# Routing of the last query items and the first expert's tokens in an attention, mixture-of-experts and softplus kernel

## The chip, the core and the metric

The kernel runs on one core of a Trainium2 chip. The metric is the device time of one execution in microseconds (us); runs of the kernel before and after the change are compared.

## The reference, cut to what matters

Three layers follow one another: a linear attention with exponential random features (4 batches, 8 heads, 576 positions, head size 64, 128 features), a mixture of experts that sends each of the 2304 tokens to one of 8 experts, and a dense layer with softplus.

```python
logits = x @ w_gate
expert_idx = np.argmax(logits, axis=1)
probs = np.exp(logits - logits.max(-1, keepdims=True))
probs /= probs.sum(-1, keepdims=True) + 1e-09
gate_w = probs[np.arange(N), expert_idx]
for e in range(E):
    mask = expert_idx == e
    h = np.maximum(x[mask] @ w1[e], 0.0)
    out[mask] = gate_w[mask, None] * (h @ w2[e])
```

Here x is the attention's output. The weight of the chosen expert is 1 / (sum of exp(logit - max) + 1e-9), as its own exponential is 1.

## The kernel before, in words

**Items.** Attention works through 20 items, numbered 0 to 19, of 256 tokens (`nr` 2) or 128 (`nr` 1): items 0 to 4 are the keys of the first two batches, 5 to 9 their queries, 10 to 14 and 15 to 19 those of the other two. The loop over `n` (from 950) runs item n's transposes and projections on TensorE (PE) beside the products of item n - 1. `at(step, slot, ...)` puts later steps of an item in a slot of a coming turn. A query item ends in products `nm` (`q_product`, 661) in PSUM banks of the tag `acc`, of which there are three; VectorE (DVE) divides them by their denominators `rc` into the token rows and, for the gate, into `lgp`.

**Routing.** Each query item goes through three steps. `route_pick` (702) sums the gate's logits `lg`, takes their maximum `rmx`, the differences `dl`, the candidates `cand`, their highest `cm` and the one-hot choice `oh`, all tiles of 128 x 16 or less in SBUF, on DVE; then it adds `oh` to the running count `run`, on GpSimd (POOL), for the last two items on DVE. `route_gate` (743) takes the exponential of `dl` on ScalarE (ACT), sums it, adds 1e-9 (L749), inverts (L750), and stores the token rows with their weight to `x_tok` in DRAM by a DMA on the queue of SyncE (SP). `route_rank` (874) multiplies `oh` by a triangle and the running counts by ones on PE (`rk`, L877 to L879), which gives each token's slot `sl` (L884) in its expert's list; POOL scatters the token's number into `id_slot` in DRAM by an indirect DMA (L906).

**The passage to the first expert.** The first expert (the fullest by items 5 to 9, chosen midway) starts before the last lists are written. `read_first` (772) reads its part of `id_slot` into `ids_0`, at the end of turn 18, behind the scatter of item 16. Item 17's tokens are added without DRAM: `add_first` (777) builds a one-hot `s0` of the slots on DVE (L782), multiplies token numbers by it on PE (`pid`, L786) and adds the result to `ids_0` on DVE (L789, L790). `gather_first` (793) then has POOL gather the rows by three indirect DMAs (L796) into `xg_0`; they also wait for item 17's store of `x_tok`. Items 18 and 19, the `tail`, never pass through DRAM for the first expert: their rows are split in two parts, `tail_h` (ACT, L752) and `tail_l` (DVE, L738), and multiplied by one-hot matrices `tail_s` of their slots in `first_tail` (810; L820, L823), which are built on ACT for item 18 (L889, L891) and on DVE for item 19 (L893). `first_split` (849) adds the gathered rows by products with diagonals of their weights (L859 on ACT, L863 on PE) into the same four PSUM tiles and splits the sum for the first expert's matmuls (L1069 to L1071). `fill` (803) puts zero products on PE in between: 4 and 4, then 3.

**What sets the order.** The text is one stream of instructions; the Tile framework gives every engine its own list in an order that its planner works out from estimated durations, with semaphores where data pass between engines. Within an engine's list, and in SP's and POOL's queues of DMAs, everything goes in that order: a waiting entry holds what is behind it. `behind(a, b)` makes the planner put a after b. From the first expert on, PE multiplies without pause by weights that SP's queue fetches.

## Time and profile before

| | |
|---|---|
| median of 3 runs | 831.66 us (830.14 to 833.51) |
| profiled execution | 830.93 us, span 829.2 us |
| mean granted clock of PE in it | 0.995 |
| busy share of the span | PE 98%, DVE 58%, ACT 57%, POOL 27% |
| attention's last product ends, first expert's first product starts | about 171.3 us, 182.1 us |

A span is the time from the first to the last instruction of an execution. Busy time is read per engine; idle time of an engine that nobody waits for costs nothing. "PEld" is PE's loading of the stationary operand, which overlaps its products. [...] "SPq" marks DMA issues of SP's queue.

### The profile page before, as it was taken

What the parts mean: (1) busy time and instruction counts of PE and PEld (TensorE: products, weight loads), DVE (VectorE), ACT (ScalarE), POOL (GpSimd) and SP (SyncE); (2) the same over time, 40 slices, a digit from 0 to 9 for tenths busy, and PEclk for the clock granted to TensorE, in tenths of its full rate; (3) what the DMA queues carried; (4) which work ended last, traced back from release to release, by engine and by line L of the source; (5) the groups of instructions that cost most, each with busy time, mean ns of one, the idle gap of its engine ahead of it and who ended that gap; (6) DMA issues with size and microseconds to landing.
All of it is one profiled execution on the core that took longest, in us unless ns stands there. A gap on an engine that the chain in (4) does not pass through costs nothing.

```text
span 829.2 us, 14048 instructions
## 1 busy us (share of the span) xinstructions
PE 813.3 (98%) x5121; PEld 756.8 (91%) x5123; DVE 484.5 (58%) x1038; ACT 473.4 (57%) x1051; POOL 227.7 (27%) x391
## 2 busy tenths in 40 slices
PE   8999999999999999999999999999999999999995
PEld 6999999979999999999999999999999999999994
DVE  6778877878777678787587666432232232222221
ACT  4787558847545545556456655664454455445442
POOL 7987898641110110110144233210000001001001
PEclk9999999999999999999999999999999999999998
DMA  9941164237777787889553220120010001001001
GB/s 258 205 131 59 33 179 160 97 102 213 221 248 246 247 272 257 276 267 311 193 157 122 77 103 1 51 102 1 1 39 38 1 1 40 1 0 39 1 1 40
DMA packets 80428, 99.29 MB, mean 120 GB/s; under 512 B 16616, under 2 KB 61832, under 8 KB 80356
## 3 DMA queue, kind: packets, MB, share of 16 engines
q1 hardware_dynamic: 76612, 88.53, 34.4%
q0 software_dynamic: 3744, 9.82, 3.5%
q8 instruction: 42, 0.69, 0.4%
q14 instruction: 30, 0.25, 0.2%
HBM read 78.59 MB, written 19.76 MB: 119 GB/s over the span
## 4 chain that ended last, share of the span: by engine, by line
PE 59%; issue 35%; POOL 2%; DVE 1%; ACT 1%; DMA 1%; SPq 0%; POOLq 0%; ACTq 0%; DVEq 0%
PE a L1069 7%; PE a L1070 7%; PE a L1071 7%; PE y L1069 4%; PE y L1071 4%; PE y L1070 4%; PE kvacc L607 3%; PE nm L670 3%; PE pj L552 2%; PE pj L556 2%; PE pj L555 2%; PE o L1366 2%; PE o L1363 2%; PE o L1368 2%; PE tq L654 2%
## 5 line engine op out<-in xcount | busy, mean ns | idle before, releaser
L1351 DVE SCALAR_TENSOR_TENSOR ab<-a,ab 128x384 f32<-128x384 f32 x96 | 53.4, 556 | 163.2 <-ACT ab L1350 163.1
L1069 PE MATMUL a<-yh,w 128*128 128x384 f32 x384 | 130.5, 340 | 0.0
L1071 PE MATMUL a<-yh,w 128*128 128x384 f32 x384 | 129.9, 338 | 0.0
L1070 PE MATMUL a<-yl,w 128*128 128x384 f32 x384 | 129.7, 338 | 0.0
L1366 PE MATMUL o<-w,gh 128*128 128x512 f32 x288 | 115.0, 399 | 0.0
L1363 PE MATMUL o<-w,gh 128*128 128x512 f32 x288 | 114.3, 397 | 0.0
L1368 PE MATMUL o<-w,gl 128*128 128x512 f32 x288 | 113.3, 394 | 0.0
L1348 ACT ACTIVATE ab<-a 128x384 f32<-128x384 f32 x96 | 47.0, 490 | 115.7 <-PE a L1071 115.7
L577 ACT ACTIVATE ph<-pj,nb 128x128 f32<-128x128 f32 x288 | 82.8, 414 | 27.8 <-DVE nb L575 17.4
L1383 POOL DMA_INDIRECT out_dram<-ob,idx x18 | 17.6, 978 | 282.5 <-ACT ob L1381 278.6
L1355 DVE TENSOR_TENSOR gl<-ab,gh 128x384 fp32r<-128x384 f32 x96 | 61.7, 643 | 52.1 <-ACT gh L1354 52.1
L290 DVE TENSOR_TENSOR w<-raw,w 128x1024 fp32r<-128x1024 f32 x64 | 78.3, 1223 | 17.4 <-ACT w L287 16.7
L1354 ACT ACTIVATE gh<-ab 128x384 fp32r<-128x384 f32 x96 | 50.5, 526 | 53.9 <-DVE ab L1351 53.6
L1071 PE MATMUL y<-hh,w 128*128 128x344 f32 (+7 forms) x256 | 77.9, 305 | 0.0
L1070 PE MATMUL y<-hl,w 128*128 128x344 f32 (+7 forms) x256 | 77.8, 305 | 0.0
L287 ACT ACTIVATE w<-raw 128x1024 fp32r<-128x1024 f32 x64 | 67.4, 1055 | 16.0 <-DMA raw<-in_moe_w_dram 16.0
L1069 PEld LDWEIGHTS a<-yh,w 128*128 128x128 f32 x384 | 72.1, 188 | 4.5
L1069 PE MATMUL y<-hh,w 128*128 128x344 f32 (+7 forms) x256 | 75.8, 306 | 0.4 <-issue 0.4
L1070 PEld LDWEIGHTS a<-yl,w 128*128 128x128 f32 x384 | 72.2, 188 | 4.1
L1071 PEld LDWEIGHTS a<-yh,w 128*128 128x128 f32 x384 | 72.0, 188 | 0.0
L1147 ACT ACTIVATE hh<-a 128x344 fp32r<-128x344 f32 (+7 forms) x64 | 27.0, 422 | 74.6 <-PE a L1071 70.9
L1069 PE MATMUL a<-xh,w 128*128 128x340 f32 (+6 forms) x224 | 68.3, 305 | 0.0
(246 smaller groups left out, 1916.7 us busy)
## 6 DMA issues: line engine op xcount, KB each, us to landing
raw<-in_moe_w_dram SPq DMA_DIRECT2D x57, 512.0 KB, 4.7
raw<-in_moe_w_in_dram SPq DMA_DIRECT2D x16, 512.0 KB, 7.5
raw<-in_moe_w_out_dram SPq DMA_DIRECT2D x16, 512.0 KB, 3.5
yb<-y_comp SPq DMA_DIRECT2D x6, 768.0 KB
vf<-in_v_dram SPq DMA_DIRECT2D x4, 1024.0 KB, 7.7
qf<-in_q_dram SPq DMA_DIRECT2D x4, 1024.0 KB, 8.0
wi_f<-cvr SPq DMA_DIRECT2D x16, 256.0 KB, 4.9
raw<-wi_f SPq DMA_DIRECT2D x8, 512.0 KB, 4.4
```

Source lines behind the costliest of these rows:

```text
L287: ins = nc.scalar.activation(slot[:, c:c + 1024], raw[:, c:c + 1024], AF.Copy)
L290: nc.vector.tensor_tensor(slot[:, 1024 + c:1024 + c + 1024], raw[:, c:c + 1024], slot[:, c:c + 1024].bitcast(F32), op=ALU.subtract)
L577: ins = nc.scalar.activation(dst[j], pj[:, j // 2, j % 2, :], AF.Exp, bias=nb[:, j // 2, j % 2:j % 2 + 1])
L1069: next_on_pe(nc.tensor.matmul(o, lhsT=wH, rhs=xH, start=first, stop=False))
L1070: next_on_pe(nc.tensor.matmul(o, lhsT=wH, rhs=xL, start=False, stop=False))
L1071: next_on_pe(nc.tensor.matmul(o, lhsT=wL, rhs=xH, start=False, stop=last))
L1351: nc.vector.scalar_tensor_tensor(ab, a, 0.0, ab, op0=ALU.max, op1=ALU.add)
L1354: placed[0] = nc.scalar.activation(gh, ab, AF.Copy)
L1355: placed[1] = nc.vector.tensor_tensor(gl, ab, gh.bitcast(F32), op=ALU.subtract)
L1363: ins = nc.tensor.matmul(os[t], lhsT=gh[:, s], rhs=u[:, c:c + DM], start=f == 0, stop=False)
L1366: nc.tensor.matmul(os[t], lhsT=gh[:, s], rhs=u[:, 1024 + c:1024 + c + DM], start=False, stop=False)
L1368: ins = nc.tensor.matmul(os[t], lhsT=gl[:, s], rhs=u[:, c:c + DM], start=False, stop=f == NF2 - 1)
```

## The change

- **Ids.** `read_first` goes to slot 0 of turn 18 and so needs item 15's scatter only; `add_first` is done for items 16 and 17, the first into `part_0`, the second from it into `ids_0`. The products `pid` come ahead of the last `nm` of item 19's first group on PE.
- **Ranks.** For items 17 to 19 no running sums are made in `route_pick`; `count_ahead` adds the earlier items' `oh` one by one in further products into `rk`, and into the final count `ct`. The slots' integer copies `si` of these items go from DVE to POOL, item 17's behind the gathers.
- **Passage.** `tail_s` is built on DVE for both tail items. `first_tail` and the products with the gathered rows, now in `first_gathered`, are put in PE's order by hand: item 18's `tail_h`, gathered block 0, item 19's rank, block 1, item 18's `tail_l`, item 19's two parts, block 2. `fill` puts 2 and 4 zero products, and the 3 of before are gone. On DVE, item 18's `lg` comes ahead of item 19's `rc`; `tail_l` of item 19 follows its `tail_s`.
- **Pick.** But for the last item of each half and the tail, `lg`, `dl` and `cand` lie in columns of the item's last `nm` bank that no product uses.
- **1e-9.** The exponentials go into one of two tiles with nine columns, the ninth set to 1e-9 once by POOL; the sum runs over nine columns and the addition L749 is gone.
- The casts of two early weight tiles on POOL are ordered behind scatters instead of running sums (`latest["run"]`).

```diff
@@ q_product @@
+                    if it is tail[1] and grp == 0:
+                        behind(latest["nm"], latest["pid"])
...
+            if grp == 2:
+                it.spare = nm[:, n * DG:512]
...
+            if it is tail[1]:
+                behind(ins, latest["lg"])
@@ gate_constants, route_pick @@
+                exs.append(sm.tile([P, 2, E + 1], F32, name=f"ex{i}", bufs=1))
+                nc.gpsimd.memset(exs[i][:, :, E:E + 1], 1e-9)
...
+            bank = not (it.last or it in tail)
+
+            def small(x, name):
+                if bank:
+                    a = it.spare[:, x * 2 * E:(x + 1) * 2 * E].rearrange("p (i e) -> p i e", i=2)
+                else:
+                    a = sm.tile([P, 2, E], F32, tag=name, name=name)
+                return a[:, 0:n]
...
+            if it in items[-3:]:
+                return
             it.ohs = sm.tile([P, 2, E], BF16, tag="ohsum", name="ohsum")
             nxt_run = sm.tile([P, E], BF16, tag="run", name="run")
-            eng = nc.vector if it in tail else nc.gpsimd
...
+        def count_ahead(dst, i, upto):
+
+            ahead = [run[0]] + [t.oh[:, j, :] for t in items[-3:][0:upto] for j in range(t.nr)]
+            ahead += [items[-3:][upto].oh[:, j, :] for j in range(i)] if upto < 3 else []
+            for x, rhs in enumerate(ahead):
+                nc.tensor.matmul(dst, lhsT=ones_b, rhs=rhs, start=upto == 3 and x == 0,
+                                 stop=upto == 3 and x == len(ahead) - 1)
@@ route_gate @@
-            nc.scalar.activation(ex, it.dl, AF.Exp)
+            nc.scalar.activation(ex[:, :, 0:E], it.dl, AF.Exp)
...
-            nc.vector.tensor_scalar(gw, gw, 1e-9, None, op0=ALU.add)
...
-            if it is tail[1]:
-                rest_of_x(it, None)
@@ add_first @@
-            part = sm.tile([P, NC], F32, tag="part", bufs=1, name="part")
-            nc.vector.tensor_tensor(part, ids_0, pid[:, :, 1], op=ALU.add)
-            nc.vector.scalar_tensor_tensor(ids_0, pid[:, :, 0], 64.0, part, op0=ALU.mult,
-                                           op1=ALU.add)
+            nc.vector.tensor_tensor(part_0, ids_0 if it is items[-4] else part_0, pid[:, :, 1],
+                                    op=ALU.add)
+            nc.vector.scalar_tensor_tensor(part_0 if it is items[-4] else ids_0, pid[:, :, 0],
+                                           64.0, part_0, op0=ALU.mult, op1=ALU.add)
@@ fill, first_gathered @@
-                zeroes(4, "tp", 2, latest["nm"])
+                zeroes(2, "tp", 2, latest["nm"])
...
+        def first_gathered(c):
...
+            ins = nc.scalar.activation(diag, ident[:, 0:w], AF.Copy, scale=xg_0[:, c, DM:DM + 1])
+            behind(ins, latest["diag"] if c == 1 else latest["rounded"])
+            latest["diag"] = ins
+            for kk in range(KD):
+                in_turn_on_pe(nc.tensor.matmul(
+                    tp_0[kk][:, c * P:c * P + w], lhsT=xg_0[:, c, kk * P:(kk + 1) * P], rhs=diag,
+                    start=False, stop=c == NC - 1))
@@ route_rank @@
-            nc.tensor.matmul(rk, lhsT=tri_b, rhs=it.oh, start=True, stop=False)
-            nc.tensor.matmul(rk, lhsT=ones_b, rhs=it.ohs[:, 0:n], start=False, stop=False)
+            ins = nc.tensor.matmul(rk, lhsT=tri_b, rhs=it.oh, start=True, stop=False)
+            if it is tail[1]:
+                behind(ins, latest["PE"])
+            if it in items[-3:]:
+                for i in range(n):
+                    count_ahead(rk[:, i, :], i, items[-3:].index(it))
...
-                    if it is tail[0]:
-
-                        nc.scalar.activation(tail_d, iota_s[:, 0:CAPS[0]], AF.Abs, scale=-1.0,
-                                             bias=sl[:, i:i + 1])
-                        nc.scalar.activation(tail_s[t], tail_d, AF.Relu, scale=-1.0, bias=1.0)
-                    else:
-                        nc.vector.tensor_scalar(tail_s[t], iota_s[:, 0:CAPS[0]], sl[:, i:i + 1],
-                                                None, op0=ALU.is_equal)
-            elif it is items[-3]:
+                    ins = nc.vector.tensor_scalar(tail_s[t], iota_s[:, 0:CAPS[0]], sl[:, i:i + 1],
+                                                  None, op0=ALU.is_equal)
+                if it is tail[1]:
+                    rest_of_x(it, ins)
+            elif it in items[-4:]:
                 add_first(it, sl)
-                gathers = gather_first()
+                if it is items[-3]:
+                    gathers = gather_first()
...
-            ins = nc.vector.tensor_copy(si[:, 0:n], sl[:, 0:n])
-            if it is tail[1]:
-                behind(ins, latest["DVE"])
-                latest["DVE"] = ins
+            eng = nc.gpsimd if it in items[-3:] else nc.vector
+            ins = eng.tensor_copy(si[:, 0:n], sl[:, 0:n])
+            if it is items[-3]:
+                behind(ins, gathers)
...
+            latest["run"] = ins
@@ the loop @@
                             at(n + 2, 1, fill, 4)
+                            at(n + 2, 1, first_tail, [(t, tail_h) for t in pv.tiles])
+                            at(n + 2, 1, first_gathered, 0)
                         if pv is tail[1]:
-                            at(n + 1, 2, fill, 3)
-                            at(n + 1, 2, first_tail, tail_t)
+                            at(n + 1, 2, first_gathered, 1)
+                            at(n + 1, 2, first_tail, [(t, tail_l) for t in tail[0].tiles])
+                            at(n + 1, 2, first_tail,
+                               [(t, x) for x in (tail_h, tail_l) for t in pv.tiles])
+                            at(n + 1, 2, first_gathered, 2)
...
-            if n == NI - 2:
-                read_first()
+            if n == NI - 3:
+                at(n + 1, 0, read_first)
...
-        nc.tensor.matmul(ct, lhsT=ones_b, rhs=run[0], start=True, stop=True)
+        count_ahead(ct, 0, 3)
```

## Rows read from the trace of the kernel before

**Rows 1.** The page, part 1: busy time of each engine, share of the span, instructions.
```profile
PE 813.3 (98%) x5121; PEld 756.8 (91%) x5123; DVE 484.5 (58%) x1038; ACT 473.4 (57%) x1051; POOL 227.7 (27%) x391
```

**Rows 2.** Table of stretches: length, busy of PE, PEld, DVE, ACT, POOL, PEclk, DMA, GB/s.
```profile
60.00:100.00 40.00, 38.29 (x334) 36.46 (x334) 35.77 (x135) 26.45 (x88) 30.24 (x64) 0.96 0.15 48
...
300.00:400.00 100.00, 100.00 (x751) 97.88 (x750) 73.99 (x117) 56.13 (x100) 9.84 (x9) 1.00 0.86 279
```

**Rows 3.** Waits of PE from 55 to 110 us: total, times, longest.
```profile
PE rk L877 <- DVE oh L720: 1.1, 2, 0.6
PE pj L552 <- ACT ph L577: 0.5, 1, 0.5
```

**Rows 4.** Timeline, 84 to 100 us: start, duration, engine, line, [idle before].
```profile
87.75 2.04 POOL L488 TENSOR_TENSOR x<-kf 128x512 f32<-128x512 f32 x2
...
88.81 1.01 DVE L713 TENSOR_TENSOR dl<-lg,rmx 128x16 f32<-128x16 f32 x1
...
90.50 0.18 PE L877 MATMUL rk<-oh,tri_b 128*128 128x16 bf16 x1 [0.62 <-DVE oh L720]
```

**Rows 5.** Table of stretches of 5 us, same columns as Rows 2.
```profile
90.00:95.00 5.00, 4.01 (x27) 3.88 (x28) 4.62 (x20) 4.09 (x14) 3.64 (x8) 0.81 0.26 105
95.00:100.00 5.00, 4.95 (x38) 4.93 (x38) 4.05 (x13) 0.79 (x4) 4.26 (x11) 0.85 0.01 0
```

**Rows 6.** Groups of DVE by form, 60 to 175 us: busy us, mean ns, idle before.
```profile
L575 DVE TENSOR_TENSOR nb<-sq,mx 128x4 f32<-128x4 f32 x18 | 6.9, 397 | 0.2
...
L713 DVE TENSOR_TENSOR dl<-lg,rmx 128x16 f32<-128x16 f32 x8 | 2.8, 355 | 0.2
...
L686 DVE SCALAR_TENSOR_TENSOR rc<-eps,nm 128x6 f32<-128x6 f32 x14 | 2.2, 157 | 0.5 <-PE nm L670 0.5
...
L749 DVE TENSOR_SCALAR xt<-xt 128x2 f32<-128x2 f32 x7 | 1.7, 242 | 0.0
...
L711 DVE TENSOR_REDUCE rmx<-lg 128x2 f32<-128x16 f32 x8 | 1.3, 159 | 0.0
```

**Rows 7.** SP's queue, 130 to 200 us: its waits, then its timeline.
```profile
SPq L774 <- DMA id_slot<-tok,si: 9.3, 1, 9.3
...
167.51 0.39 SPq L774 DMA_DIRECT2D ids<-id_slot  x1
168.00 0.43 SPq L763 DMA_DIRECT2D x_tok<-xt  x1
```

**Rows 8.** DMA issues, 140 to 200 us: count, KB each, median us to landing.
```profile
x_tok<-xt SPq DMA_DIRECT2D x3, 513.0 KB, 3.7
...
tail<-x_tok,ids POOLq DMA_INDIRECT x3, 3.9
```

**Rows 9.** Timeline of the passage, 158 to 182 us.
```profile
165.31 0.16 DVE L750 RECIPROCAL xt<-xt 128x2 f32<-128x2 f32 x1
...
168.16 0.74 DVE L782 TENSOR_SCALAR s<-iota_s,sl 128x384 bf16<-128x384 f32 x2
...
169.94 0.28 PEld L786 LDWEIGHTS <-s 128*128 128x128 bf16 x5
...
171.28 0.15 DVE L790 SCALAR_TENSOR_TENSOR ids<-pid,part 128x3 int32<-128x3 f32 x1
...
172.62 1.06 POOL L796 DMA_INDIRECT tail<-x_tok,ids  x1 [6.12 <-DVE cm L718]
...
173.61 0.16 DVE L884 TENSOR_REDUCE sl<-t 128x2 f32<-128x16 f32 x1
...
175.55 0.43 PE L820 MATMUL xtp<-tail 128*128 128x344 f32 x1 [0.60 <-ACT tail L891]
...
175.62 0.39 DVE L893 TENSOR_SCALAR tail<-iota_s,sl 128x344 fp32r<-128x344 f32 x1
...
177.90 0.40 ACT L859 ACTIVATE diags<-ident,tail 128x128 f32<-128x128 f32 x1 [0.36 <-DMA tail<-x_tok,ids]
...
179.45 2.81 PE L863 MATMUL xtp<-diags,tail 128*128 128x128 f32 x24
```

More of the change, by code (lines that the diff above doesn't have):

```diff
@@ L700, in tile_favor_moe_softplus, with gate_constants @@
         run = [ohsum]
+        exs = []
+        def gate_constants():
+            for i in range(2):
+                exs.append(sm.tile([P, 2, E + 1], F32, name=f"ex{i}", bufs=1))
+                nc.gpsimd.memset(exs[i][:, :, E:E + 1], 1e-9)
         def route_pick(it):
@@ L706, in bc @@
                 return a.rearrange("p (i o) -> p i o", o=1).to_broadcast([P, n, last])
-            lg = sm.tile([P, 2, E], F32, tag="lg", name="lg")[:, 0:n]
-            nc.vector.tensor_reduce(lg, it.lgp[:, 0:n], axis=AX.X, op=ALU.add)
+            bank = not (it.last or it in tail)
[5 more added lines that the diff above has]
+                return a[:, 0:n]
+            lg = small(0, "lg")
+            latest["lg"] = nc.vector.tensor_reduce(lg, it.lgp[:, 0:n], axis=AX.X, op=ALU.add)
             mx = sm.tile([P, 2], F32, tag="rmx", name="rmx")[:, 0:n]
             nc.vector.tensor_reduce(mx, lg, axis=AX.X, op=ALU.max)
-            it.dl = sm.tile([P, 2, E], F32, tag="dl", name="dl")[:, 0:n]
+            it.dl = small(1, "dl")
             nc.vector.tensor_tensor(it.dl, lg, bc(mx), op=ALU.subtract)
-            cand = sm.tile([P, 2, E], F32, tag="cand", name="cand")[:, 0:n]
+            cand = small(2, "cand")
             nc.vector.scalar_tensor_tensor(
@@ L744, in route_gate @@
             n = it.nr
[L745 to L746 removed]
+            ex = exs[turns.index(it) % 2][:, 0:n]
+            nc.scalar.activation(ex[:, :, 0:E], it.dl, AF.Exp)
             gw = it.xg[:, 0:n, DM]
             nc.vector.tensor_reduce(gw, ex, axis=AX.X, op=ALU.add)
[L749 removed]
             nc.vector.reciprocal(gw, gw)
@@ L799, in gather_first, with in_turn_on_pe, first_tail @@
             return ins
-        tp_0 = []
+        part_0 = sm.tile([P, NC], F32, name="part", bufs=1)
+        tp_0, diags = [], []
         def fill(n):
             if "filled" not in latest:
-                zeroes(4, "tp", 2, latest["nm"])
+                zeroes(2, "tp", 2, latest["nm"])
             latest["filled"] = n
             zeroes(n, "tp", 2, latest["PE"])
-        def first_tail(tiles):
+        def in_turn_on_pe(ins):
+            behind(ins, latest["PE"])
+            latest["PE"] = ins
+        def first_tail(halves):
             n = CAPS[0]
@@ L816, in first_tail @@
                            for kk in range(KD)]
-            for t in tiles:
+            for t, half in halves:
                 for kk in range(KD):
                     ks = slice(kk * P, (kk + 1) * P)
-                    ins = nc.tensor.matmul(tp_0[kk][:, 0:n], lhsT=tail_h[t][:, ks], rhs=tail_s[t],
-                                           start=t == tail_t[0], stop=False)
-                    behind(ins, latest["PE"])
-                    ins = nc.tensor.matmul(tp_0[kk][:, 0:n], lhsT=tail_l[t][:, ks], rhs=tail_s[t],
-                                           start=False, stop=False)
-                    behind(ins, latest["PE"])
+                    in_turn_on_pe(nc.tensor.matmul(
+                        tp_0[kk][:, 0:n], lhsT=half[t][:, ks], rhs=tail_s[t],
+                        start=half is tail_h and t == tail_t[0], stop=False))
+        def first_gathered(c):
+            if not diags:
+                diags.append(wk.tile([P, H * 2 * D], F32, tag="x2", bufs=1, name="diags"))
+            w = min(P, CAPS[0] - c * P)
+            diag = diags[0][:, c * P:c * P + w]
+            ins = nc.scalar.activation(diag, ident[:, 0:w], AF.Copy, scale=xg_0[:, c, DM:DM + 1])
+            behind(ins, latest["diag"] if c == 1 else latest["rounded"])
+            latest["diag"] = ins
+            for kk in range(KD):
+                in_turn_on_pe(nc.tensor.matmul(
+                    tp_0[kk][:, c * P:c * P + w], lhsT=xg_0[:, c, kk * P:(kk + 1) * P], rhs=diag,
+                    start=False, stop=c == NC - 1))
         def count_first():
@@ L854, in first_split @@
             tp = tp_0
-            diags = wk.tile([P, H * 2 * D], F32, tag="x2", bufs=1, name="diags")
-            for c in range(NC):
-                w = min(P, n - c * P)
-                diag = diags[:, c * P:c * P + w]
-                ins = nc.scalar.activation(diag, ident[:, 0:w], AF.Copy,
-                                           scale=xg_0[:, c, DM:DM + 1])
-                behind(ins, latest["rounded"])
-                for kk in range(KD):
-                    nc.tensor.matmul(tp[kk][:, c * P:c * P + w],
-                                     lhsT=xg_0[:, c, kk * P:(kk + 1) * P], rhs=diag,
-                                     start=False, stop=c == NC - 1)
             for it in tail:
```

21 lines of the change are left out of this document (11 added, 10 removed).

## The prediction

> **What bounds the kernel now.** I read the page first: TensorE (PE) is busy for 98% of the span [rows 1], so the end moves only with the time in which PE stands still, or works at a lower clock. The table of stretches says where that is [rows 2]: from 300 to 400 us, among the experts, PE is busy for all 100 us; in the first q stage, 60 to 100 us, it is busy for 38.29 of 40 us at a granted clock of 0.96. Whatever starts the experts earlier therefore ends the kernel earlier by the same amount, and there are two places to look at: that q stage, and the passage from attention to the first expert.
>
> In the q stage the waits name the cause [rows 3]: PE's own waits there are two for `oh`, the last step of a pick (1.1 us), and one for an exponential (0.5 us). The timeline shows the larger one [rows 4]: GpSimd (POOL) starts squaring at 87.75 and works for 2.04 us; VectorE's (DVE) `dl` of item 8, 16 elements wide, starts at 88.81 and takes 1.01 us; and PE's `rk` (L877), next in PE's order, starts at 90.50 after standing still for 0.62 us. After those gaps the clock falls: the mean granted clock is 0.81 and then 0.85 in the two stretches of 5 us from 90 to 100 [rows 5], with PE busy for 4.01 of 5 us in the first. [...]
>
> The groups by form tell which DVE steps are stretched in this way [rows 6]: `dl` takes 355 ns in the mean (the one above 1014), the 1e-9 addition 242 ns, and `nb`, four elements, 397 ns; `rmx`, which reads one tile only, stays at 159 ns, and `rc`, which takes one operand from PSUM and one from SBUF, at 157 ns for all its 14. A small step with two SBUF operands, or a `tensor_scalar` in SBUF, waits for POOL; a step with one operand in PSUM does not.
>
> In the passage SP's queue comes first [rows 7]. The reading of the first expert's ids stood at the head of that queue for 9.3 us, until item 16's scatter had landed, and was issued at 167.51; item 17's store of x, queued behind it, went out at 168.00, although its last operand was written at 165.31 + 0.16 = 165.47 [rows 9]. A store takes 3.7 us to land and a gather 3.9 [rows 8]. So the store lands near 168.00 + 0.43 + 3.7 = 172.1 and the first gather goes out at 172.62, while its ids were ready at 171.28 + 0.15 = 171.43 [rows 9]: the store's landing, not the ids, released it.
>
> PE's side: the first selection matmul (L820) starts at 175.55, after a wait of 0.60 us for ACT's `tail_s`; the slots it is built from were ready at 173.61 + 0.16 = 173.77. From 175.55 to 179.45 PE does 24 such matmuls (0.16 us each) and then 2.81 us of diagonal products, to 182.26 [rows 9].
>
> **Part by part.** *Pick in PSUM, ninth column.* Seven of the ten picks (items 5 to 8 and 15 to 17) get `lg`, `dl` and `cand` in PSUM; item 9 and the two tail items keep SBUF. By `rc`, the nearest row, the new `dl` and `cand` take 0.16 us whatever POOL does, so the waits of 1.1 us for `oh` go. With `dl` 0.85 us shorter, the `nb` and exponentials behind it come earlier too, and the wait of 0.5 us for an exponential goes. Without 1.6 us of standing still the fall of the clock (1.7 us) should not come. That is 1.1 + 0.5 + 1.7 = 3.3 us; the other end is 0, if other collisions take their place. I take 3.3, because each of the three follows from a row of item 8 or its like. The 1e-9 addition (0.24 us, ten times) leaves DVE, mostly behind the pick; with DVE busy for 35.77 of 40 us [rows 2] its seven places in front of other picks and maxima are worth between 0 and 1.7 us to PE, and I take 0.3, since PE stands still for only 1.7 us of that stage in all. The two memsets on POOL happen once, long before.
>
> *Ids read behind item 15, ids of item 16 added.* This adds, for item 16, what L782 and L786 do for item 17: two steps of 0.37 us, two small ones of 0.15 us, on DVE 1.04 us in all, and six products, 0.06 us each [rows 9]. DVE has a tenth of its time free by the stage shown [rows 2]; the bounds for the end are 0 and 1.04 us, and I take 0.2. The moved read now waits only for item 15's scatter; on SP it stands ahead of items 16's and 17's stores, and what it costs them is bounded by its landing. The first of the two additions needs the ids that were read; DVE waits for them if they are late, with the pick and the `nb` of the next items behind it. The store of item 17 can go at 165.5 and land near 165.5 + 0.4 + 3.7 = 169.6, so the gathers are released by the ids, at 171.4 at the latest. The rank of item 17 no longer needs POOL's sums, and its products can stand closer together, so I put the first gather at 171.0, between 169.7 and 172.6.
>
> *The passage on PE.* `tail_s` of item 18 comes from one DVE step of 0.39 us behind the slots, not from two ACT steps: ready near 174.2 instead of 175.5. PE's order is now: rank of 18, four zero products, 8 matmuls of item 18 (1.3 us), the first gathered block (a third of 2.81, 0.94 us), rank of 19, second block, the other 16 matmuls (2.5 us), third block. The ranks count with more, smaller products: two more for item 17, and some 13 more in the passage, 0.7 us at 0.056 each. By tail_s alone the end would be 182.26 - 1.35 + 0.7 = 181.6. By the gathers: PE stands behind the first block until it has landed (3.9) and its diagonal is made (0.40 on ACT, about 0.5 with the handing over), and has 0.94 + 0.4 + 0.94 + 2.5 + 0.94 = 5.7 us to do after that: start + 10.1, which is 181.1 for a start at 171.0, 179.8 for 169.7 and 182.7 for 172.6. Four small DVE steps also leave the stretch ahead of item 18's slots (three of the tail's sums, the 1e-9), 0.16 us each by `rmx` [rows 6], so that this end moves to about 181.0. The later of the two, 181.1, is 1.1 us earlier than now; bounds 2.4 earlier and 0.5 later. What is late next is the first gather's landing. Seven fewer zero products cost nothing where the order leaves PE other work; if it does not, the clock falls as above (1.7 us).
>
> *Sum.* -3.3 (pick and clock) - 0.3 (ninth column) - 1.1 (passage) + 0.2 (item 16's ids) = -4.5 us. The profiled execution took 830.93 us with a span of 829.2, 0.7 us below the median of 831.66; on the median this gives 827.2.
>
> [...]
>
> **The rivals.**
> (a) *Collisions move.* `nb` stays in SBUF (18 of 397 ns here), and with another order POOL's long steps meet other DVE steps; PE still stands still near 90 us and the clock still falls. Then the passage and at most the waits for `oh` remain: -1.1 - 0.5 + 0.2 = -1.4, and 830.3 on the median. For it: the rows show that the stretched step is a matter of timing. Against: the step that held PE here is a `dl`.
> (b) *The passage gives nothing.* The gathers still start near 172.6, behind the second `ids` addition or POOL's own queue (the scatters of item 16 and a cast of weights): +0.5 there, -3.3 - 0.3 + 0.2 beside it: 828.8. For it: the ids now pass through two additions; against it: the first of them lies a whole item earlier.
> (c) *Slower: PE waits in order for the first gathered block.* Item 19's rank, its `tail_s` and 16 matmuls now stand behind that block on PE, where before only 8 products waited for the last one. From a first gather later than 172.1 each us costs one. Were it at 174.5 (late ids hold the DVE addition, POOL's queue does the rest), the block starts at 178.9, PE stands still for over 3 us from 175.5, and the clock falls: +2.4 + 1.7. With the pick giving nothing this is 835.8. Against it: the store and the ids both move to earlier, not later.
> [...]
>
> **How the numbers follow.** About 0.5% (4.2 us) is what a measurement of this kernel can tell from no change; the three runs spread over 3.4 us. The forecast has a chance of 0.60, (a) 0.18, (b) 0.09, (c) 0.08, (d) 0.05. The forecast's own range goes from all its gains at their better bounds but the ninth column's, 831.66 - 3.3 - 0.3 - 2.4 = 825.7, less the 1.5 us by which the lowest run lies under the median, 824.2, up to 829.5. The bound of faster by 0.5% is 827.5, just above its likeliest value, so some six tenths of it are faster (0.36), and of (b), with its passage a little better, half (0.05): 0.41. Slower by over 0.5% is (c): 0.08. The rest is the same: 0.51. The range takes in (a), (b) and (d) and leaves out (c) and the far ends: 824.2 to 832.0.
>
> **What would show it.** Right: `dl` and `cand` near 0.16 to 0.2 us in all items of the list, no gap of PE ahead of L877 near 90 us, a granted clock of 1.00 from 60 to 180 us; the read of ids issued before 162, item 17's store at about 165.5, the first gather before 171.5, the last diagonal product ending near 181. Wrong: a clock below 1.00 anywhere in the q stages or in the passage, PE standing still in front of the first gathered block for more than 1 us, a DVE wait for the ids read, or a first gather at 172 or later.

## The result and the profile after

The changed kernel took 836.56 us (median of 7 executions, 835.63 to 837.91) against 831.66 us (7, 830.12 to 833.85) of the kernel before: 1.0053 times as long, interval 1.0034 to 1.0072. That is 4.9 us more; the forecast was 827.2, 4.5 less, and its range ended at 832.0. The profiled execution took 837.27 us, 835.3 of it span.

Part 1 of the page answers to [rows 1]:

```profile
PE 814.9 (98%) x5139; PEld 758.1 (91%) x5141; DVE 486.1 (58%) x1026; ACT 472.0 (56%) x1047; POOL 227.9 (27%) x393
```

The table of stretches answers to [rows 2, 5], in its columns; the last two stretches are new.

```profile
60.00:100.00 40.00, 39.10 (x353) 37.09 (x354) 34.79 (x129) 28.63 (x95) 30.11 (x64) 1.00 0.14 48
90.00:95.00 5.00, 4.49 (x40) 4.13 (x38) 4.14 (x19) 4.51 (x16) 4.11 (x9) 1.00 0.01 3
95.00:100.00 5.00, 4.89 (x42) 4.76 (x42) 4.68 (x14) 1.58 (x6) 4.26 (x10) 1.00 0.27 105
180.00:185.00 5.00, 2.11 (x8) 1.77 (x8) 2.11 (x5) 0.00 (x0) 2.20 (x4) 0.77 0.82 158
185.00:190.00 5.00, 5.00 (x22) 5.00 (x22) 4.24 (x13) 1.74 (x4) 0.14 (x1) 0.54 0.00 0
```

The first q stage looks as forecast: 0.8 us more of PE, clock 1.00 (that the clock is no gain of the change is shown below). The loss is in the passage: from 180 to 185 us PE is busy for 2.11 of 5 us, and then works at 0.54 of full speed. Its timeline (start, duration, engine, line, in brackets the idle time before and its releaser), engine by engine put in one order of time:

```profile
172.42 1.02 POOL L822 DMA_INDIRECT tail<-x_tok,ids  x1 [6.79 <-DVE cand L736]
...
176.21 0.40 ACT L862 ACTIVATE diags<-ident,tail 128x128 f32<-128x128 f32 x1 [1.93 <-DMA tail<-x_tok,ids]
176.51 0.19 ACT L774 ACTIVATE ex<-dl 128x8 f32<-128x8 f32 x1
176.74 0.16 DVE L776 TENSOR_REDUCE own<-ex 128x1 f32<-128x9 f32 x1 [0.93 <-ACT ex L774]
177.07 0.17 DVE L741 TENSOR_TENSOR oh<-cand,cm 128x8 bf16<-128x8 f32 x1
177.16 1.41 DVE L766 SCALAR_TENSOR_TENSOR tail<-own,tail 128x512 fp32r<-128x512 f32 x2
177.91 0.17 PE L917 MATMUL rk<-base_b,ones_b 128*128 128x8 bf16 x1
...
181.23 0.47 PE L852 MATMUL xtp<-tail 128*128 128x344 f32 x2 [1.14 <-issue]
182.82 0.17 DVE L920 TENSOR_TENSOR t<-rk,oh 128x8 f32<-128x8 f32 x1 [4.25 <-remote]
183.22 0.41 DVE L925 TENSOR_SCALAR tail<-iota_s,sl 128x344 fp32r<-128x344 f32 x1
183.77 2.63 PE L852 MATMUL xtp<-tail 128*128 128x344 f32 x8 [1.48 <-DVE tail L925]
186.20 1.84 PE L866 MATMUL xtp<-diags,tail 128*128 128x88 f32 x8
187.76 0.92 PE L1110 MATMUL a<-w,w 128*128 128x344 f32 x2
```

`t` is the step of DVE that takes the ranks `rk` out of PSUM; the slots `sl`, the matrices `tail_s` and item 19's matmuls on PE follow from it. Two things stand there. ACT's diagonal of the first gathered block is queued ahead of item 19's exponential, and DVE's sum of that exponential ahead of the pick's last steps, so `oh` of item 19 comes at 177.07. In the kernel before:

```profile
173.73 0.17 DVE L720 TENSOR_TENSOR oh<-cand,cm 128x8 bf16<-128x8 f32 x1
174.11 0.17 PE L879 MATMUL rk<-base_b,ones_b 128*128 128x8 bf16 x1
```

And DVE's `t` of item 19, which waits for PE's rank, starts at 182.82, though the rank's last product ended at 177.91 + 0.17 = 178.08 and DVE was free at 178.57: the release is **4.25 us late**. PE itself stands still there for 1.14 us without any wait that the profile shows.

Where the time went by stage, worked out from the starts of the first and last q products (`nm`) and of the first expert's first product in five traces (columns 2, 3 and 4 are experiments below):

```
us                                    before  before_p  pick_dve   again   after
up to the first q product              50.60     50.78     50.58   52.68   52.61
first half's q products                47.01     45.62     44.48   44.72   44.80
up to the second half's first          36.26     36.64     37.52   36.69   36.71
second half's q products               37.15     37.02     36.74   38.18   38.20
up to the first expert's first         11.11     11.08     10.63   10.21   15.44
from there to the end                 647.07    647.46    647.85  647.02  647.54
span                                   829.2     828.6     827.8   829.5   835.3
```

The change wins 2.2 us in the second line, and loses 2.0 in the first, 1.05 in the fourth, 4.3 in the fifth, and not quite half a microsecond in each of the others.

### The profile page after: what moved, and what is told of

Read it like the earlier page. It is cut to its first block, busy times and chain, and to the rows that moved or that the text cites. A ratio compares the mean times of both kernels' runs of the same rounds, so it can differ in the third digit from the quotient of the medians.

```text
span 835.3 us, 14078 instructions
## 1 busy us (share of the span) xinstructions
PE 814.9 (98%) x5139; PEld 758.1 (91%) x5141; DVE 486.1 (58%) x1026; ACT 472.0 (56%) x1047; POOL 227.9 (27%) x393
## 4 chain that ended last, share of the span: by engine, by line
PE 56%; issue 35%; DVE 2%; POOL 2%; ACT 2%; DMA 2%; another core or an unknown queue 1%; SPq 0%; POOLq 0%; ACTq 0%; DVEq 0%
PE a L1110 7%; PE a L1111 7%; PE a L1112 6%; PE y L1110 4%; PE y L1112 4%; PE y L1111 4%; PE nm L670 3%; PE kvacc L607 3%; PE pj L552 2%; PE o L1407 2%; PE o L1404 2%; PE o L1409 2%; PE pj L556 2%; POOL out_dram L1424 2%; PE pj L555 2%
```

## The experiments

Kernels run together share a chip and the timed executions of the kernel before. There were five such occasions after the result: (1) again, sums, pick_only, rank_first; (2) again5, pick_dve, after_dve, ids_late; (3) sums_b, scatter_late, early_dve; (4) again6, sums_c, double, pick_dve_b; (5) before_p, bursts_pick, best. The kernel before itself took 832.1 and 832.2 us on occasions 2 and 4 and 830.7 to 831.0 on the others, so times are set beside times of the same occasion. Ratios are to the kernel before, with their 95% interval. Of the theories named by letters in the expectations, T holds the bursts of small counting products to be what delays PE's semaphore, D the transfers of the passage; the others are told where they first stand.

**The changed kernel again** (no edit; again, again5, again6).

> The changed kernel, unaltered, profiled once more. Theory S (something that belongs to this order of instructions): the release of DVE's t of item 19 (L920) is again about 4 us later than the end of the rank's last product (L917), PE again shows gaps of over 1 us between 179.5 and 184, the clock falls there, the first expert starts near 187.8, 836 to 838 us. Theory A (an accident of that one execution): the release follows within 0.1 us, the first expert starts near 183.5, and the other executions of 836 us must have lost their time elsewhere.

> The changed kernel unaltered, timed five rounds, since its second profile (831.4 us, first expert's first product at 182.48) lacks the loss of the first one (837.27 us, 187.76). Theory C (the 4 to 5 us come with the occasion on which the kernel was measured, and the kernel itself is no slower than before): 830.5 to 832.5 us, at most one or two executions above 834, interval around 1.000. Theory S (the kernel loses them in most executions and the second profile was a lucky one): a median of 835 us or more.

> The changed kernel unaltered, beside the next two on the same occasion. Theory T and theory D alike: on an occasion with late releases 834 to 837 us and t of item 19 late by 1 to 5 us; on one without, 831 to 832 us.

again took 831.4 us, one execution, and its passage has no late release (below); again5 834.86 (832.74 to 837.24), ratio 1.0038 [1.0022, 1.0053]; again6 835.74, 1.0048 [1.0032, 1.0065]. The profiled execution of again5 is its fastest: `t` of items 18 and 19 comes 1.54 and 1.24 us late there, and the first expert's product at 183.30.

```profile
178.26 0.16 DVE L920 TENSOR_TENSOR t<-rk,oh 128x8 f32<-128x8 f32 x1
178.45 0.16 DVE L922 TENSOR_REDUCE sl<-t 128x1 f32<-128x8 f32 x1
...
182.48 0.58 PE L1110 MATMUL a<-w,w 128*128 128x344 f32 x2
```

In again6 the first profile's loss is there once more, at the same place, the first expert's product at 186.96:

```profile
174.38 0.17 DVE L920 TENSOR_TENSOR t<-rk,oh 128x16 f32<-128x16 f32 x1 [0.58 <-PE rk L917]
...
182.62 0.17 DVE L920 TENSOR_TENSOR t<-rk,oh 128x8 f32<-128x8 f32 x1 [4.24 <-PE ct L760]
```

So the same program loses 2.8 to 4.9 us on three occasions (the result's, 2 and 4) and nothing in its one execution on occasion 1: the first half of A's outcome there, nearly S's in again5, which misses its 835 by 0.14. The traces themselves tell the occasions apart. DVE's updates of its semaphore are recorded to within two of about 1000 in the traces of occasions 1 and 5 and in that of the kernel before on which the prediction rests; in those of the result and of occasions 2 to 4, 23 to 39 of them are missing (970 recorded of 1000 in the result's). Between 172 and 183 us the former hold 68 to 104 records of landed transfers, the latter 17 to 61 (20 in the result's), with the same transfers under way. The chip alone does not decide it: occasions 2 and 5 carry the same chip number. Where records are missing PE's updates can come late; where they are complete, no rank's update came over 0.1 us late in any trace. This table has the traces with missing records, in us from the end of the rank's last product to the record of PE's update (`t` is late by less where DVE had other work until later):

```
                 item 18  item 19            item 18  item 19
result              0.74     4.72   ids_late    0.01     2.10
again5              1.79     1.22   early_dve   0.02     0.93
again6              0.82     4.66   sums_b      0.01     0.64
double              1.63     3.84   sums_c      0.01     2.14
scatter_late        0.72     1.72   pick_dve    0.02   (under 1.2)
after_dve           0.03     5.03   pick_dve_b  0.01     0.01
```

The kernel before was not traced on such an occasion; pick_dve and pick_dve_b have its order of the passage.

**The pick alone** (pick_only, pick_dve, pick_dve_b; before_p is the kernel before, unaltered). pick_only is the kernel before with these parts of the diff; pick_dve also has the last line:

```diff
+            if grp == 2:
+                it.spare = nm[:, n * DG:512]
...
-            it.dl = sm.tile([P, 2, E], F32, tag="dl", name="dl")[:, 0:n]
+            it.dl = small(1, "dl")
...
-            nc.vector.tensor_scalar(gw, gw, 1e-9, None, op0=ALU.add)
...
-                nc.gpsimd.memset(exs[i][:, :, E:E + 1], 1e-9)
+                nc.vector.memset(exs[i][:, :, E:E + 1], 1e-9)
```

> The kernel before with the pick's three small tiles in PSUM and the ninth column, and nothing else. The prediction's two steps say 3.6 us less: no fall of the clock near 93 us, 828.0 us (827 to 829). Rival (collisions move): a fall of the clock elsewhere in the q stages, 830 to 832 us. If these two parts themselves were what made the change slower: 834 us or more.

> The kernel before with the pick in PSUM and the ninth column, the two 1e-9 memsets on VectorE instead of POOL. Theory P (the two memsets on POOL tip the planner's order of the k stage: nb of one item behind a maximum, the exponentials late, PE standing still for 1.1 us at 33 us): no such gap, first q product near 50.6 instead of 52.4, the first expert's first product at 179.3 to 180 instead of 181.04, 828.5 to 830 us. Rival (the time won there is lost again behind the transfers of the passage, whose first gather stays at 172): first product at 181 to 182 and 830.5 to 831.5 us.

> The kernel before with the pick in PSUM, the ninth column and its two memsets on VectorE, once more. By its first profile (first expert's first product at 179.95 against 182.13, the end 1.4 us earlier): 0.998 to 0.9995 of the kernel before. Rival (the experts after the first give it all back): 1.000.

> The kernel before, unaltered, profiled beside the next two. Theory X (PE's updates come late only for a rank that stands among the landings of the gathers, after 175): t of items 18 and 19 released within 0.2 us on any occasion, first expert's first product near 182. If the kernel before has late releases too, of 1 us or more, the position is not what tells them apart.

pick_only: 830.98 us, 1.0007 [0.9992, 1.0023]; pick_dve: 831.10, 0.9993 [0.9978, 1.0007]; pick_dve_b: 831.82, 0.9989 [0.9974, 1.0005]; before_p: 830.43, its releases on time. pick_only misses its 828.0, and pick_dve its 828.5 to 830; both profiled executions are the fastest of their twelve. In pick_only the first q product came at 52.37, in pick_dve at 50.58, and the first expert's first product at 181.04 and 179.95 (before: 182.13). In pick_dve_b they came at 51.05 and 181.91, with a span of 829.1. Theory P is shown for the k stage: only the engine of two memsets differs between pick_only and pick_dve, and with it the planner's order. Of DVE around 31 us, first the changed kernel, then pick_dve:

```profile
32.46 0.69 DVE L574 TENSOR_REDUCE mx<-pj 128x4 f32<-128x512 f32 x1 [0.76 <-PE pj L556]
33.06 1.27 DVE L575 TENSOR_TENSOR nb<-sq,mx 128x4 f32<-128x4 f32 x3
```

```profile
31.22 0.41 DVE L575 TENSOR_TENSOR nb<-sq,mx 128x4 f32<-128x4 f32 x2
32.06 0.69 DVE L574 TENSOR_REDUCE mx<-pj 128x4 f32<-128x512 f32 x1 [0.43 <-PE pj L556]
```

pick_only has the first order (maximum at 32.31, three `nb` from 32.92), the kernel before the second. With the memsets on POOL two `nb` go behind the next maximum; ACT's exponentials wait for them (2.80 us), and PE for the exponentials, a wait that pick_dve's k stage at 33 us does not have:

```profile
PE kvacc L607 <- ACT ph L577: 1.1, 1, 1.1
```

The memsets themselves take nothing: 0.25 us on an idle POOL at 8.03 us.

before_p shows the other half. In its trace the clock does not fall in the first q stage, though PE stands still as in [rows 5], and its waits from 55 to 110 us are those of [rows 3], 1.1 and 0.5 us:

```profile
90.00:95.00 5.00, 3.88 (x33) 3.56 (x33) 4.79 (x22) 4.45 (x16) 3.50 (x8) 1.00 0.26 105
95.00:100.00 5.00, 4.95 (x45) 4.94 (x44) 4.51 (x14) 1.02 (x5) 4.26 (x11) 1.00 0.01 0
```

So the fall that the prediction took out was that of one execution. Against before_p the pick wins 45.62 - 44.68 = 0.9 us in pick_only and 45.62 - 44.48 = 1.1 us in pick_dve, not 3.3. The k stage behind is as long in pick_only as in before_p (36.61 and 36.64 us), but 37.52 in pick_dve: moving the memsets to VectorE wins 1.8 us in the first k stage and gives 0.9 back in the second. As far as the mean clock of an execution tells it (0.995 in the prediction's, 0.996 here), most look like before_p: 34 of the 143 timed executions of the kernel before on the five occasions have 0.995 or less. The 1.2 to 2.2 us by which pick_dve's experts start earlier than in before_p and before become 0.8 to 1.4 in the span; pick_dve_b's start 0.8 us later than before_p's. In the medians no gain is clear of the interval.

**The ids and the memsets in the changed kernel** (ids_late, after_dve). after_dve has only the last line of the diff above; ids_late this:

```diff
-            elif it in items[-4:]:
+            elif it is items[-3]:
                 add_first(it, sl)
-                if it is items[-3]:
-                    gathers = gather_first()
+                gathers = gather_first()
...
-            if n == NI - 3:
-                at(n + 1, 0, read_first)
+            if n == NI - 2:
+                read_first()
```

> The changed kernel with the ids read behind item 16 as before, and only item 17's ids added. Theory I (the second round of ids sums delays the q stage of the last items by about 1.5 us: last q product at 172.3, against 170.4 with the pick alone, and the earlier store wins nothing, as it lands at 171.7 all the same): last q product at 170.5 to 171, first gather at 171.5 to 172.2, first expert's first product 0.5 to 1 us earlier than 182.48. Rival R (the early ids do bring the gather forward): the first gather goes out at 172.6 or later and the first product moves to 182.7 or later.

> The changed kernel with the two memsets on VectorE and nothing else. Theory P: first q product near 50.7 instead of 52.6, last q product near 170.5 instead of 172.3, first gather near 170.7 instead of 172.6, first expert's first product near 180.7 instead of 182.48, 829 to 830 us. Rival: the first gather stays at 172 (item 17's store decides, and its landing does not move), first product at 182 or later, 831 us.

ids_late: 833.52 us, 1.0011 [0.9996, 1.0026], beside again5's 1.0038. The last q product came at 170.74 in place of 172.06, so theory I's first half holds: the second half's q products take 36.70 us, against 38.2 with both rounds of sums. But the first gather went out at 172.76 (again5: 171.82), as R said: without the early read item 17's store is issued at 168.74 in place of 166.51, and the gather follows the store. In time ids_late is 1.3 us under again5, with intervals that overlap, so that nothing is decided. after_dve: 835.11, 1.0032 [1.0020, 1.0045]. Its q stages are earlier (first q product 51.02, last 171.14, gather 171.42), nearly as P says, but `t` of item 19 was released 4.47 us late, and the first expert's product came at 186.57: what is won ahead of the passage is lost in it.

**What makes the release late** (sums, sums_b, sums_c, double, bursts_pick, scatter_late). The sums kernels count as the kernel before does (the steps of the running sums on POOL and DVE, not shown, come back too):

```diff
-            if it in items[-3:]:
-                for i in range(n):
-                    count_ahead(rk[:, i, :], i, items[-3:].index(it))
-            else:
-                nc.tensor.matmul(rk, lhsT=ones_b, rhs=it.ohs[:, 0:n], start=False, stop=False)
+            nc.tensor.matmul(rk, lhsT=ones_b, rhs=it.ohs[:, 0:n], start=False, stop=False)
...
-        count_ahead(ct, 0, 3)
+        nc.tensor.matmul(ct, lhsT=ones_b, rhs=run[0], start=True, stop=True)
```

double adds to `count_ahead`, for the ranks, a product with zeros behind each:

```diff
+                if upto < 3:
+                    nc.tensor.matmul(dst, lhsT=ones_b, rhs=zero_b[:, 0:E], start=False, stop=False)
```

bursts_pick puts `count_ahead`, as the change has it, into pick_dve. scatter_late takes the tail's scatters out of the passage, not those of item 17:

```diff
+            if it in tail:
+                it.sl = sl
+                return
+            scatter_ids(it, sl, gathers if it is items[-3] else None)
...
+            for it in tail:
+                scatter_ids(it, it.sl, None)
             return xh, xl
```

> The changed kernel with running sums again for items 17 to 19 (POOL and DVE steps, one ones_b product per rank and one for ct) in place of the bursts of small counting products. Theory T (the bursts of small products hold up PE and its semaphore): the late release of L920 and PE's gaps near 180 are gone, the first expert starts near 183.5 to 184, 832 to 833 us. Theory O (what costs is the order of the passage, item 19's pick and rank behind the first gathered block): nothing of that moves, 835.5 to 837 us.

> The kernel with running sums in place of the bursts of small counting products once more, since it has run only on the occasion on which the changed kernel lost nothing either. On an occasion on which PE's updates of its semaphore come late (to be seen in the profile: DVE's t of item 18 or 19 over 1 us behind the rank's last product): theory T (the bursts cause it) says t follows within 0.2 us and the ratio to before is 1.000 to 1.002; theory D (it comes with the transfers of the passage, whatever PE does) says the release is late by 1 to 5 us all the same and the ratio is 1.003 to 1.005. On an occasion without it: 1.000 as before, and nothing is told apart.

> The changed kernel with running sums in place of the bursts of small products, beside the unaltered one. Theory T (the bursts delay PE's semaphore): t of items 18 and 19 within 0.2 us of rank or of DVE being free, 3 to 5 us less than the unaltered kernel on an occasion with late releases, 831 to 832.5 us. Theory D (the transfers do): within 1 us of the unaltered kernel. On an occasion without late releases both theories give no difference over 0.5 us.

> The changed kernel with each small counting product of the last three ranks followed by another one of zeros (15 more, the sums unaltered). Theory T: the releases of t of items 18 and 19 come later still, by 1 us or more than with the unaltered kernel, and 1 to 4 us more in the time; late even on an occasion on which the unaltered kernel's are not. Theory D: only PE's own time for 15 more products, 0.03 us each, 0.4 us in all.

> The changed kernel with the casts and scatters of the last two items' slots put behind the first expert's split, out of the passage. Theory D1 (the scatters, 128 descriptors of 4 bytes each, are the transfers that hold up PE's semaphore): on an occasion with late updates they are gone, first expert's first product at 182 to 183; the ids of the second expert come later, which may cost 0 to 3 us behind it. Theory D2 (the gathers do it) and theory T: the release of t of item 19 is late as before. Without late updates: first product at 182.5 and what the later scatters cost.

> The kernel pick_dve (kernel before, pick in PSUM, ninth column, memsets on VectorE) with the bursts of small counting products in place of the running sums of items 17 to 19, the order of the passage as in the kernel before: ranks at 172 to 173, ahead of the gathers' landings. Theory T (a burst delays PE's semaphore wherever it stands): on an occasion with late releases t of item 18 or 19 is late by 1 us or more, and 1.002 or more of the kernel before. Theory X (only among the landings): within 0.2 us, and 0.998 to 1.000 as without the bursts.

sums, on the occasion without late releases: 831.37 us, 1.0000 [0.9991, 1.0009], as again; nothing told apart. sums_b: 831.59, 1.0013 [1.0003, 1.0022], `t` on time, while scatter_late beside it, with the bursts, had them 0.47 and 1.33 us late. (The table has an update of sums_b 0.64 us late; DVE was busy until then.) sums_c beside again6: 832.60, 1.0004 [0.9988, 1.0020], that is 835.74 - 832.60 = **3.1 us less**, the intervals apart. Its releases were not all on time:

```profile
179.50 0.17 DVE L915 TENSOR_TENSOR t<-rk,oh 128x8 f32<-128x8 f32 x1 [1.56 <-remote]
...
184.07 0.59 PE L1105 MATMUL a<-w,w 128*128 128x344 f32 x2 [1.25 <-issue]
```

double: 835.05 us, 1.0021 [1.0005, 1.0037], `t` 1.31 and 3.87 us late: item 18's later than in again6 (0.58), item 19's not, and no more time in all. So that the bursts cost some 3 us is shown on one such occasion, and item 18's update was late only with bursts (in five of eight traces); that each small product adds its share is not shown, and T falls in that form. Without bursts item 19's update can still be late (2.14 us), so they are not all of the cause. scatter_late: 835.17 (4 executions), 1.0053 [1.0038, 1.0068]. The late releases stayed (1.33 us), so the tail's scatters are not needed for them; but item 17's two, issued at 176.32 and 177.63, stayed in the passage too, and D1 is not settled for these. Its first expert's product came at 182.66; the time went behind it, where PE waited 1.9 us for the second expert and the rest took 650.75 us (again: 647.06). bursts_pick: 831.90, 1.0020 [1.0004, 1.0036], releases on time, but on an occasion with complete records, so X is not tried where it matters.

**The order of the passage** (rank_first, early_dve, best). rank_first puts the first gathered block behind item 19's gate and rank; early_dve also puts item 18's matmuls there, and has the memsets on VectorE; best is early_dve with running sums and ids_late's edit.

```diff
                             at(n + 2, 1, fill, 4)
-                            at(n + 2, 1, first_tail, [(t, tail_h) for t in pv.tiles])
-                            at(n + 2, 1, first_gathered, 0)
                         if pv is tail[1]:
+                            at(n + 1, 2, first_tail, [(t, tail_h) for t in tail[0].tiles])
+                            at(n + 1, 2, first_gathered, 0)
                             at(n + 1, 2, first_gathered, 1)
```

> The changed kernel with the first gathered block (its diagonal on ACT and its products on PE) put behind item 19's gate and rank, in place of ahead of them. Theory O (order): oh of item 19 comes at about 174.3 in place of 177.1, its rank before 177, tail_s of 19 before 178, no idle PE over 0.6 us after 176, clock 1.00, the first expert's first product at 182 to 183, 831 to 832.5 us. Theory T (small products): the release of t of item 19 is late by about 4 us all the same, and PE, with some 3.5 us of other products in between, still stands still: 834 us or more.

> The changed kernel with the two memsets on VectorE and, in the passage, item 19's rank right behind item 18's (before all gathered blocks and before item 18's matmuls), as in the kernel before. Theory O (a rank behind the first gathered block is what exposes PE to the transfers and puts a chain of DVE and PE steps at the end): t of item 19 before 175, no PE gap over 0.5 us between 175 and 182, first expert's first product at 179.5 to 180.5, ratio 0.997 to 0.999 on any occasion. Rival (late updates strike the earlier rank as well, or the first gathered block's landing decides): first product at 181.5 or later, ratio 1.000 or more.

> The changed kernel without the parts that the runs found to cost time: memsets on VectorE, running sums in place of the bursts, item 19's rank right behind item 18's, the ids read behind item 16 and only item 17's added; left of the change are the pick in PSUM, the ninth column, tail_s of item 18 on DVE and the gathered blocks between the tail's matmuls. First q product at 50.6 to 51.1, last q product at 169.3 to 169.8, first expert's first product at 179.3 to 180.5, 0.997 to 0.999 of the kernel before. Rival (the first gather and the second expert's gather set the time, as with pick_dve): 0.999 to 1.000.

rank_first: 831.59 us, 1.0004 [0.9992, 1.0017], no different from again or sums. Its profile shows O's mechanism, smaller than O has it: `oh` of item 19 at 175.25 (again: 176.85), first expert's product at 181.86 (182.48). That execution took 651.5 us from there to the end, 4.5 us more than again: the second expert's gather came late:

```profile
PE xtp L1142 <- DVE cum L1307: 1.9, 1, 1.9
PE xtp L1142 <- ACT xg L1134: 0.8, 1, 0.8
```

rank_first ran on an occasion with complete records, so T was not tried by it.

early_dve: 831.23, 1.0007 [0.9995, 1.0018], first product at 182.24: the forecast 179.5 to 180.5 was missed. But it has the bursts, ran on an occasion with missing records, and is level there. With the rank early, DVE was still busy with item 18's rest when the update arrived (176.63, 0.93 us late), and PE had other matmuls to do. That the early rank is what saved it is argued, not shown: the changed kernel itself did not run on that occasion. best: 831.66, 1.0014 [1.0001, 1.0027], a miss: PE waited 1.7 us for `oh` of item 19, and the first product came at 182.34. No version beats the kernel before beyond its interval; pick_dve comes nearest.

## Why the prediction was wrong, step by step

**Pick in PSUM, -3.3: right mechanism, mis-sized.** The groups of DVE by form, to be laid beside [rows 6] (`nm` as output is the tile in the bank; busy us, mean ns):

```profile
L736 DVE SCALAR_TENSOR_TENSOR nm<-nm,desc 128x16 f32<-128x16 f32 x6 | 1.1, 181 | 0.2
L734 DVE TENSOR_TENSOR nm<-nm,rmx 128x16 f32<-128x16 f32 x6 | 1.1, 178 | 0.1
L732 DVE TENSOR_REDUCE rmx<-nm 128x2 f32<-128x16 f32 x6 | 1.0, 168 | 0.1
...
L734 DVE TENSOR_TENSOR dl<-lg,rmx 128x16 f32<-128x16 f32 x2 | 0.6, 286 | 0.0
...
L732 DVE TENSOR_REDUCE rmx<-lg 128x2 f32<-128x16 f32 x2 | 0.3, 168 | 0.0
```

`dl` takes 178 ns where it took 355 (164 to 182 each in the bank, with POOL at work or not; 411 for item 9's, in SBUF beside a step of POOL), and PE's wait for `oh` from 55 to 110 us fell from 1.1 to 0.2 us:

```profile
PE rk L909 <- DVE oh L741: 0.2, 1, 0.2
```

That a step is dearer when it reads PSUM, which was rival (d), no run shows: `rmx` takes 168 ns from either memory, and its chance of 0.05 and its place in the range had no measured number behind them. The term that was mis-sized is the clock: 5 x 0.19 + 5 x 0.15 = 1.7 us of full speed, by [rows 5], were measured in one execution, and before_p has none of it with the same waits (a clock of 1.00 from 90 to 100 us), so the step "Without 1.6 us of standing still the fall of the clock (1.7 us) should not come" took for a consequence what comes in one execution and not in another. What is left against before_p is 0.9 to 1.1 us.

**Ninth column, -0.3, with its memsets at nothing: the step that failed first.** "The two memsets on POOL happen once, long before" looked for their cost on POOL. They moved `nb` in the planner's order, 25 us later on another engine, and cost 1.8 us up to the first q product (52.37 - 50.58, pick_only against pick_dve; 1.3 against pick_dve_b). By the second half's first q product, after what is given back in the k stage, 133.66 - 132.58 = 1.1 us are left (0.6 against pick_dve_b). The column's own gain was not measured apart.

**Item 16's ids, +0.2: mis-sized.** It is 1.5 us (38.2 against 36.70 in ids_late, which also reads the ids later), above the bound of 1.04, in which only DVE's steps stood; the six products (0.36) were counted and then left out of it.

**Passage, -1.1: the first gather's input did not hold.** The read went out early (156.95) and nothing waited for it. Item 17's store went out at 166.77 in place of 168.00, but landed at 171.49, in the kernel before at 171.69:

```profile
156.95 0.37 SPq L799 DMA_DIRECT2D ids<-id_slot  x1
...
166.77 0.34 SPq L788 DMA_DIRECT2D x_tok<-xt  x1
```

Of its 16 landing records eight stand at 170.30 to 170.38 and eight at 171.20 to 171.49, 4.7 us after the issue where [rows 8] have 3.7. So the first gather went out at 172.42, 0.93 us behind that landing as in the kernel before, and not at 171.0: rival (b)'s outcome, by the landing it took for granted. From the gather to the end of the last diagonal product again takes 182.61 - 172.62 = 10.0 us, beside the 10.1 of the formula; the result takes 15.6.

**The step that lost the time, +4 to 5 us: "start + 10.1".** This sum has, behind the first block's landing, only PE's own 5.7 us of work. It puts the chain from item 19's rank on PE through `t`, `sl` and `tail_s` on DVE back to PE at nothing, without a reason. On time the chain fits in (again); late it is added whole. Rival (c) named the place, item 19's rank behind the first gathered block, and nearly the number (835.8), but for a late gather. The gather was not late. Late was `oh` of item 19, behind the block through ACT's and DVE's queues (177.07 against 173.73 before), and above all PE's update behind the rank. The kernel before has its rank of item 19 at 174.1 (row above), with all of item 18's matmuls still to come; in the changed kernel the eight matmuls of item 19 and the last block wait for it at the end, so that of 4.25 us of lateness 5 - 2.11 = 2.9 us from 180 to 185 became idle PE, and the clock fell with it: 5 x 0.23 + 5 x 0.46 = 3.4 us of full speed, by the two stretches from 180 to 190 us. Without the late release the change wins nothing either: again ends 0.3 us behind the profiled kernel before and 0.9 behind before_p, in one execution; sums, the change but for its bursts, has 1.0000.

**Chances.** The forecast of 0.60 rested on three terms of one execution. "Slower" had 0.08, all of it hung on a late gather.

## What to carry to other kernels

A gain read from one trace should first be looked for in a second trace of the same kernel: a fall of the clock is not in every execution (here 0.81 from 90 to 95 us in one, 1.00 in the other). An instruction that costs nothing on its engine (here two memsets, 0.25 us on an idle POOL) still enters a planner's order, so compare the order of all engines before and after, from the first row that differs. Where a chain PE, DVE, PE is moved to the end of a passage, count what PE still has to do while it runs: that is the lateness it can bear; of 4.25 us here, 2.9 became idle PE.

## What was not expected of the hardware

PE's update of a semaphore can reach DVE up to 5.0 us after the product's end (after_dve; on time it takes 10 to 30 ns), on occasions on which records of updates and of landings are also missing from the trace. What holds it back is open: the bursts of small products add to it (3.1 us of time, again6 against sums_c), the tail's scatters are not needed for it (1.33 us without them in the passage, scatter_late), and 2.1 us of it came without bursts (sums_c). Why records are missing (of landings between 172 and 183 us the result's trace has 20, that of the kernel before 79), and whether PE's updates are late for the same reason, no run shows. Every execution here is a recorded one, with a span and a clock, so whether an unrecorded one has the delay cannot be told.

A store issued 1.2 us earlier landed 0.2 us earlier: half of its parts came 0.8 to 1.2 us behind the other half. In the kernel before the second half came 0.5 to 0.9 us behind, and the other traces have 3.1 (pick_dve) to 5.0 us (again) from issue to landing. Whether other transfers under way, such as item 16's scatters, make the difference was not tried.
